# Two-stage kernel on one core (windowed attention, then a gated feed-forward): the loads of the first quad and of the first global rows

## The chip, the cores and the metric

The kernel runs on 1 core of one Trainium2 chip. The time is the device time of one execution in microseconds (us); the time before is the median of 3 runs. One further execution was profiled, and every view below is of that one.

A core has five engines that work side by side, each in its own program order: PE (TensorE, matmul; the loading of the stationary operand is shown apart, as PEld), DVE (VectorE), ACT (ScalarE), POOL (GpSimd) and SP (SyncE). They meet only at semaphores. Transfers between HBM and the on-chip memory are issued from SP, ACT or POOL and carried out by 16 DMA engines. The profile calls the queue of the transfers that POOL issues q0 ("software_dynamic"), that of SP q1 and that of ACT q10 (both "hardware_dynamic"). Only transfers issued from POOL change the type on the way here (f32 in HBM, bf16 on chip); those from SP and ACT bring f32 as it is.

## The reference, cut to what matters

```python
# q_l, k_l, v_l: (8, 8, 512, 64); q_g, k_g, v_g: (8, 8, 32, 64); all f32
def _attn_ref(q_l, k_l, v_l, q_g, k_g, v_g):
    k_all = np.concatenate([k_g, k_l], axis=2)
    v_all = np.concatenate([v_g, v_l], axis=2)
    out_g = np.matmul(sm(scale * q_g @ k_all.T), v_all)       # 32 global queries see every key
    mask = np.abs(pos[:, None] - pos[None, :]) <= 32          # local queries: a band of 65 keys
    s_ll = np.where(mask, scale * q_l @ k_l.T, -1e9)
    s_l = np.concatenate([scale * q_l @ k_g.T, s_ll], axis=-1)  # and the 32 global keys
    out_l = np.matmul(sm(s_l), v_all)
    return np.concatenate([out_g, out_l], axis=2)

def _moe_ref(x, w_in, w_out):                                 # x: (4352, 512)
    h = x @ w_in                                              # 512 -> 2048
    return (h / (1.0 + np.exp(-1.702 * h))) @ w_out           # 2048 -> 512
```

`sm` is a softmax over the last axis. The attention output, with the heads put side by side, is the input x of the feed-forward.

## The kernel before, in words

**Tiling.** The 8 batches are cut into 16 "quads" of four heads each: quad Q is batch Q // 2, heads 4(Q % 2) to 4(Q % 2) + 3. The first two quads (batch 0, called `a` and `c` in the code) are of class `Quad`, the other fourteen of class `Wide`. Per quad, k and q arrive as bf16 tiles `rk` and `rq` (128 x 1024), are turned on DVE by stream transposes into `kT` (`Tk`, L304 to L309) and a q tile `qt` (`Tq`, L311 to L313), and scores are made on PE (`S`). There are four such q tiles (`qtiles`, L181 to L186), each 128 x 24 x 32; the middle 16 of the 24 columns hold the local queries, and copies of the global queries are put into the outer columns by `ext` (L319 to L327). The class `Quad` has its own `ext`, with a switch that puts a copy on ACT instead of DVE; `Wide` has another one, which the change does not touch.

**The order of the work** is written out by hand: each engine does its instructions in the order in which the program makes them. For batch 0 that order is L653 to L737. In short, for quad a: scores of round 0 in two parts (`a.S(0, part=0)`, `part=1`), their exponential on ACT (`a.X(0)`, L387), round 1 (`a.S(1)`, `a.X(1)`, L382), then the transposes of quad c, its bias matmuls `c.B(0)` (L337), the products with global keys (`a.K`, `a.XK`, L373 and L418), `c.S(0)`, `c.X(0)`, the sums and products with v (`ekU`, `U`, L428 and L440), normalisation on DVE (`R`, `XL`, L464 to L473), and the same for c. Between them PE is given filler matmuls on a zeroed tile (`zero`, L648, and L179 at the start). When quad a's rows are normalised, the feed-forward of batch 0 begins (L713, `h_mm`, L588); it needs `w_in_sb`, which POOL loads in eight pieces (L256). From there the program alternates feed-forward (`h_step`, `o_mm`) with the attention of the next batch.

**The first loads.** Before the main order, each issuing engine gets its transfers, in this order:

- SP: global queries of batch 0 into `g32q` (L132, 64 KB, f32); the second half of quad 0's q into `early[:, 2]` (L146, 256 KB, f32); global keys into a buffer of their own, `g32k` (L132).
- ACT: quad 0's k in two halves into `early[:, 0:2]` (L144, 2 x 256 KB, f32).
- POOL: the first half of quad 0's q straight into `rq` (L145, 128 KB as bf16); the constant `step` by an `affine_select` (L153); then quad 1's k and q (`load(0, (1,), "kq")`, L81, 256 KB each as bf16), global values (L117, L118), the local values of batch 0 in four pieces (L243), some constants, and the weights (L256, L246).

The f32 pieces are turned into bf16 on chip: `cast_k` (L651) does the two halves of k on ACT, L658 the half of q on ACT, and `cast_g32` (L135) the global queries and keys on DVE. The casts and transposes in the hand-written order are L653 to L665: k on ACT; global queries on DVE (cast, then `transpose_g`, L237); the first two of quad a's four `ext` copies on ACT; q's half on ACT; `a.Tk` in two halves, `a.Tq` in two halves, the other two `ext` copies, and the cast and transpose of the global keys, all on DVE. Quad c's `Tk`, `Tq` and its four `ext` copies on DVE follow at L678 to L681.

The tile `early` is used once more, from L724 on, as the place of a tanh of the feed-forward.

Of the kernel before, what the change touches and what calls it, by code (L numbers as in the profile page):

```python
# [12 lines left out]
F32 = mybir.dt.float32  # L13
BF16 = mybir.dt.bfloat16
FP8 = mybir.dt.float8e4
AF = mybir.ActivationFunctionType
# [4 lines left out]
def kernel(  # L21
# [12 lines left out]
    nc = tc.nc  # L34

    B, H, Sl, D = q_l.shape
# [12 lines left out]
    TB = 512  # L49
# [7 lines left out]
    consts = ctx.enter_context(tc.tile_pool(name="consts", bufs=1))  # L57
    wts = ctx.enter_context(tc.tile_pool(name="wts", bufs=1))
    ld = ctx.enter_context(tc.tile_pool(name="ld", bufs=3))
# [6 lines left out]
    qf = q_l.rearrange("b (u j) (r t) d -> b (j r) u (t d)", j=4, t=16)  # L66
    kf = k_l.rearrange("b (u j) (r t) d -> b (j r) u (t d)", j=4, t=16)
    qgf = q_g.rearrange("b (u j) s d -> (j s) (b u) d", j=4)
    kgf = k_g.rearrange("b (u j) s d -> (j s) (b u) d", j=4)
# [4 lines left out]
    def load(b, us=(0, 1), names="qk"):  # L74
        if b not in loaded:
            loaded[b] = (ld.tile([128, 2, 16 * D], BF16, name="rk"),
                         ld.tile([128, 2, 16 * D], BF16, name="rq"))
        s = slice(us[0], us[-1] + 1)
        for name in names:
            dst, src = ((loaded[b][0], kf), (loaded[b][1], qf))[name == "q"]  # L80
            nc.gpsimd.dma_start(out=dst[:, s], in_=src[b][:, s])  # L81
# [34 lines left out]
    def load_turned(eng, out_, in_):  # L116
        eng.dma_start(out=out_[32:128], in_=in_[0:96])  # L117
        eng.dma_start(out=out_[0:32], in_=in_[96:128])  # L118
# [5 lines left out]

    g32 = {}

    def load_g32(name, src):
        t = g32[name] = consts.tile([128, 2, D], F32, name="g32%s" % name)
        if name == "v":
            load_turned(nc.sync, t, src[:, 0:2, :])  # L130
        else:
            nc.sync.dma_start(out=t, in_=src[:, 0:2, :])  # L132

    def cast_g32(name, t):
        nc.vector.tensor_copy(t[:, 0:2, :D], g32[name])  # L135

    load(0, names="")
    rk, rq = loaded[0]
    early = ld.tile([128, 4, TB], F32, name="early", bufs=1)
    k32 = early[:, 0:2].rearrange("p a b -> p (a b)")  # L140
    halves = (slice(0, 8 * D), slice(8 * D, 16 * D))
    load_g32("q", qgf)
    for f in halves:
        nc.scalar.dma_start(out=k32[:, f], in_=kf[0][:, 0, f])  # L144
    nc.gpsimd.dma_start(out=rq[:, 0, halves[0]], in_=qf[0][:, 0, halves[0]])  # L145
    nc.sync.dma_start(out=early[:, 2], in_=qf[0][:, 0, halves[1]])  # L146
    load_g32("k", kgf)

    warm = consts.tile([128, 512], BF16)
    nc.vector.memset(warm, 0.0)  # L150
# [3 lines left out]
        out=step, in_=step, pattern=[[1, 289]], compare_op=ALU.is_ge,  # L154
        fill=0.0, base=-97, channel_multiplier=-1,
    )
    ones32 = consts.tile([128, 32], BF16)
    bd = consts.tile([128, 4, 32], BF16)
    for i in range(2):
# [21 lines left out]
    qtiles = []  # L181
    for i in range(4):
        qt = consts.tile([128, 24, 32], F32, name="q%d" % i)
        nc.vector.memset(qt[:, 0:4, :], 0.0)
        nc.vector.memset(qt[:, 20:24, :], 0.0)
        qtiles.append(qt)  # L186

    qgT = consts.tile([128, NQ, 40], F32)
# [44 lines left out]
    def transpose_g(lo, hi, names="qk"):  # L233
        for name, dst, s in (("q", qgT, rqg), ("k", kgT, rkg)):
            if name not in names:
                continue
            nc.vector.transpose(dst[:, lo:hi, :32], s[:, lo:hi].bitcast(F32))  # L237
# [404 lines left out]
    pts, th4s = {}, {}  # L642

    a, c = Quad(0), Quad(1)
# [2 lines left out]
        for _ in range(n):  # L647
            nc.tensor.matmul(ps[:m, :w], lhsT=warm[:, :m], rhs=warm[:, :w], start=False, stop=False, skip_group_check=True)  # L648

    def cast_k(f):  # L650
        nc.scalar.activation(rk[:, 0, f], k32[:, f], AF.Copy)  # L651

    cast_k(halves[0])  # L653
    cast_k(halves[1])
    cast_g32("q", rqg)
    transpose_g(0, 2, "q")
    a.ext((0, 1), True)
    nc.scalar.activation(rq[:, 0, halves[1]], early[:, 2], AF.Copy)  # L658
    a.Tk(0, 8)
    a.Tk(8, 16)  # L660
    a.Tq(0, 8)
    a.Tq(8, 16)
    a.ext((2, 3))
    cast_g32("k", rkg)
    transpose_g(0, 2, "k")  # L665
    load_rest()
# [9 lines left out]
    zero(16, a.bk[1][3], 32, 32)  # L676
    a.X(1)
    c.Tk()  # L678
    c.ext((0, 1))
    c.Tq()  # L680
    c.ext((2, 3))  # L681
    c.B(0)
    a.K()
    a.XK()
# [36 lines left out]
            h_mm(0, fc, bank(pt, fc), (kc,))  # L721
    a.G()
    c.Gm()
    th4 = th4s[0] = early  # L724

    def tanh2(hf):
        f = slice(2 * hf, 2 * hf + 2)
# [16 lines left out]
    a, c = nq[1]  # L744
# [41 lines left out]
    a, c = nq[2]  # L786
# [122 lines left out]
```

## Time and profile before

| what | us |
|---|---|
| median of 3 runs | 299.23 (299.15 to 299.37) |
| the profiled execution, device time | 299.14 |
| its span, first to last instruction | 297.4 |
| PE busy in the span | 289.9 |
| DVE busy | 218.7 |
| ACT busy | 165.5 |
| POOL busy | 81.9 |

The granted TensorE clock is 1.0 over the whole span. Busy PE time includes the filler matmuls. In the timeline view a row is: start in us, length in us, engine, source line, operation, output <- inputs, shape, how many, and in brackets the idle time of the engine before it and what ended that. In the DMA view a queue's row is: packets, MB, and the time its packets took as a share of 16 engines in the stretch that was asked for; "to landing" is from the start of the issuing instruction to the moment the transfer is complete. Landings of the first transfers, as that view and the rows of single tiles give them (us after the issue, issue time in brackets):

| transfer | issued | to landing |
|---|---|---|
| k half 0, ACT, 256 KB f32 | 0.82 | 3.0 |
| global queries, SP, 64 KB f32 | 0.82 | 3.1 |
| q second half, SP, 256 KB f32 | 1.34 | 4.8 |
| global keys, SP, 64 KB f32 | 1.84 | 5.9 |
| q first half, POOL, 128 KB bf16 | 1.32 | 5.4 |
| quad 1's k, POOL, 256 KB bf16 | 2.48 | 5.7 |
| quad 1's q, POOL, 256 KB bf16 | 3.04 | 6.5 |

### The profile page before, as it was taken

The page shows a single profiled execution, that of the slowest core. Times are in us where ns is not written, and L with a number is a line of the kernel's source. Part 1 is how long each engine was busy: PE and PEld are TensorE (multiplying, and loading weights), DVE is VectorE, ACT ScalarE, POOL GpSimd, SP SyncE. Part 2 cuts the span into 40 slices and gives each one's busy share as a digit, 9 for nine tenths or more (in the row PEclk, how much of TensorE's full clock was granted, in tenths as well). Part 3 has the DMA queues.
Part 4 walks back from the last instruction along what each step waited for, and adds up shares of the span by engine and source line. Part 5 has one row for each costly group of instructions (what it writes and reads, how often), then busy time and mean ns, then how long its engine had stood idle before and what let it go on. Part 6 is the DMA issues. An engine that isn't in the chain of part 4 may idle for free.

```text
span 297.4 us, 8162 instructions
## 1 busy us (share of the span) xinstructions
PE 289.9 (97%) x3403; PEld 149.8 (50%) x3444; DVE 218.7 (74%) x440; ACT 165.5 (56%) x252; POOL 81.9 (28%) x133
## 2 busy tenths in 40 slices
PE   8999999999999999999999999999999999999995
PEld 4544446445454455445454455445544455445653
DVE  6679888979867887778877887788878866683320
ACT  4827465585556745576447654666546651663421
POOL 8884630589565002700072003500000000000000
PEclk9999999999999999999999999999999999999999
DMA  7999994596999613961299115901130022101122
GB/s 177 178 206 211 204 160 86 119 138 100 192 212 160 124 37 68 150 122 29 47 96 178 29 41 87 109 0 39 36 72 2 2 48 63 35 2 35 35 66 78
DMA packets 59316, 28.06 MB, mean 94 GB/s; under 512 B 47376, under 2 KB 49808, under 8 KB 59280
## 3 DMA queue, kind: packets, MB, share of 16 engines
q0 software_dynamic: 51728, 17.70, 53.1%
q1 hardware_dynamic: 7264, 9.31, 12.3%
q8 instruction: 27, 0.44, 0.6%
q10 hardware_dynamic: 288, 0.52, 0.5%
q14 instruction: 9, 0.07, 0.1%
HBM read 36.31 MB, written 8.91 MB: 152 GB/s over the span
## 4 chain that ended last, share of the span: by engine, by line
PE 92%; POOL 3%; DMA 3%; issue 1%; ACT 0%; POOLq 0%
PE op L613 39%; PE hp L588 38%; PE s L533 6%; PE ov L559 5%; DMA w_in_sb<-in_moe_w_in_dram 3%; PE s L588 1%; PE op L625 1%; POOL v L243 1%; PE og L570 1%; POOL w_in_sb L256 0%; PE s L559 0%; POOL rq L145 0%; POOL rvg L117 0%; PE og L458 0%; POOL rvg L118 0%
## 5 line engine op out<-in xcount | busy, mean ns | idle before, releaser
L613 PE MATMUL op<-w_out_sb,gT 128*128 128x512 bf16 x497 | 119.4, 379 | 1.8 <-issue 0.3
L596 DVE SCALAR_TENSOR_TENSOR gT<-th,hp 128x512 bf16<-128x512 f32 (+1 forms) x140 | 91.0, 656 | 39.7 <-ACT th L595 38.7
L588 PE MATMUL hp<-xL,w_in_sb 128*128 128x512 bf16 x488 | 108.4, 379 | 0.4
L595 ACT ACTIVATE th<-hp 128x512 f32<-128x512 f32 (+1 forms) x140 | 79.8, 573 | 43.0 <-PE hp L588 41.1
L588 PEld LDWEIGHTS <-w_in_sb 128*128 128x128 bf16 x576 | 56.1, 98 | 64.2 <-issue 0.5
L613 PEld LDWEIGHTS <-gT 128*128 128x128 bf16 x528 | 49.3, 98 | 54.9
L544 ACT ACTIVATE e<-s 128x1016 bf16<-128x1016 f32 (+1 forms) x56 | 53.3, 1005 | 7.4 <-PE s L533 7.1
L628 ACT ACTIVATE ob<-op 128x512 f32<-128x512 f32 x32 | 18.9, 599 | 62.3 <-PE op L613 62.3
L97 POOL DMA_DIRECT2D v<-in_v_l_dram x35 | 28.1, 806 | 82.1 <-PE og L570 74.0
L549 DVE TENSOR_TENSOR e<-e,mask 128x1712 bf16<-128x1712 bf16 (+1 forms) x27 | 28.4, 1051 | 3.4 <-ACT e L544 3.4
L464 DVE STREAM_TRANSPOSE sT<-ov 128x512 f32<-128x512 f32 x15 | 10.7, 716 | 14.4 <-PE ov L559 12.6
L473 DVE TENSOR_TENSOR xL<-ov,rs 128x512 bf16<-128x512 f32 x30 | 19.4, 686 | 1.9 <-PE ov L440 0.5
L533 PE MATMUL s<-q,kT 32*128 32x160 bf16 (+3 forms) x672 | 19.2, 243 | 0.0
L533 PEld LDWEIGHTS <-kT 32*128 32x128 bf16 x672 | 13.1, 94 | 12.0 <-issue 6.9
L507 DVE STREAM_TRANSPOSE kT<-rk 128x512 f32<-128x512 f32 x14 | 14.5, 1035 | 0.7 <-DMA rk<-in_k_l_dram 0.7
L99 POOL DMA_DIRECT2D v<-in_v_g_dram x24 | 14.1, 586 | 0.6 <-issue 0.5
L468 DVE STREAM_TRANSPOSE rs<-rT 128x512 f32<-128x512 f32 x16 | 11.4, 711 | 0.6
L559 PE MATMUL ov<-e,v 128*32 128x128 bf16 (+3 forms) x624 | 11.7, 223 | 0.0
L312 DVE STREAM_TRANSPOSE q<-rq 128x512 f32<-128x512 f32 (+1 forms) x17 | 11.4, 672 | 0.1
L559 PEld LDWEIGHTS <-v 128*32 128x32 bf16 x672 | 10.5, 97 | 0.0
L588 PE MATMUL hp<-xG,w_in_sb 128*128 128x256 bf16 x64 | 9.6, 273 | 0.1
L81 POOL DMA_DIRECT2D rk<-in_k_l_dram x10 | 6.4, 639 | 2.6 <-DMA w_out_sb<-in_moe_w_out_dram 2.0
(103 smaller groups left out, 158.8 us busy)
## 6 DMA issues: line engine op xcount, KB each, us to landing
out_dram<-ob SPq DMA_DIRECT2D x128, 64.0 KB, 1.8
v<-in_v_l_dram POOLq DMA_DIRECT2D x28, 96.0 KB, 4.8
rq<-in_q_l_dram POOLq DMA_DIRECT2D x5, 512.0 KB, 6.5
rk<-in_k_l_dram POOLq DMA_DIRECT2D x5, 512.0 KB, 8.5
w_in_sb<-in_moe_w_in_dram POOLq DMA_DIRECT2D x8, 256.0 KB, 8.6
w_out_sb<-in_moe_w_out_dram POOLq DMA_DIRECT2D x4, 512.0 KB, 11.1
v<-in_v_l_dram POOLq DMA_DIRECT2D x11, 128.0 KB, 6.4
rk<-in_k_l_dram POOLq DMA_DIRECT2D x5, 256.0 KB, 9.1
```

The source lines that it names most:

```text
L97: nc.gpsimd.dma_start(out=vt[0:n, :, c, :D], in_=vs[FIRST[c] : FIRST[c] + n])
L473: nc.vector.tensor_mul(self.x[:, 2 * self.u + h, :], self.st[1 + h], self.st["rs"])
L507: nc.vector.transpose(flat[:, 0:Sl].rearrange("p (r t) -> p t r", t=16), loaded[self.b][0][:, self.u].bitcast(F32))
L533: nc.tensor.matmul(bank(self.ps, j)[:, at : at + n], lhsT=self.k[p, KEYS[c] : KEYS[c] + 128, e], rhs=self.q[p, lo:hi, r0 : r0 + nr, e], st ...
L544: nc.scalar.activation(self.E[rnd][:, 2 * i : 2 * i + 2, :n], self.ps[i][:, :, :n], AF.Exp, scale=scale)
L549: eng.tensor_mul(e, e, mask[:, rnd : rnd + 1, :n].to_broadcast([128, 4, n]))
L559: nc.tensor.matmul(ov[32 * j : 32 * j + 32, :].rearrange("p (t r) -> p t r", t=16)[:, t0:t1, r0 : r0 + nr], lhsT=lv, rhs=self.E[rnd][:, j, ...
L588: nc.tensor.matmul(hp[:, : width(i)], lhsT=w_in_c[:, fc // 8, kc, fc % 8 // 2, :, fc % 2], rhs=(xL[i] if i < B else xG)[:, kc, :], start=( ...
L595: nc.scalar.activation(th[:, :n], hp[:, :n], AF.Tanh, scale=0.851)
L596: nc.vector.scalar_tensor_tensor(gTs[i][:, fc, :n], in0=th[:, :n], scalar=1.0, in1=hp[:, :n], op0=ALU.add, op1=ALU.mult)
L613: nc.tensor.matmul(op, lhsT=gTs[i][:, fc, tci * 128 : tci * 128 + 128], rhs=w_out_sb[:, fc, :], start=(first and fc == 4 * f4), stop=(fc = ...
L628: nc.scalar.activation(ob, op, AF.Copy, scale=0.5)
```

## The change

Quad 0's k is loaded by POOL in one transfer with the cast to bf16, ahead of everything else on POOL; its q by POOL in two halves, right behind the `affine_select`. The f32 detours in `early`, the transfers on ACT's queue and the three casts on ACT go. Global queries and keys share one f32 buffer, `stage`: the transfer of the keys is issued on SP only after the cast of the queries, since it overwrites what that reads. The eight `ext` copies of quads a and c are done on ACT, all of them ahead of quad a's transposes in program order; `a.Tk` is one transpose instead of two halves. The eight memsets of the q tiles' outer columns on DVE go. `early` is allocated later, for the tanh alone.

```diff
+    stage = consts.tile([128, 2, D], F32, name="stage")
+
     def load_g32(name, src):
-        t = g32[name] = consts.tile([128, 2, D], F32, name="g32%s" % name)
-        if name == "v":
-            load_turned(nc.sync, t, src[:, 0:2, :])
-        else:
-            nc.sync.dma_start(out=t, in_=src[:, 0:2, :])
+        g32[name] = stage
+        nc.sync.dma_start(out=stage, in_=src[:, 0:2, :])
...
-    early = ld.tile([128, 4, TB], F32, name="early", bufs=1)
-    k32 = early[:, 0:2].rearrange("p a b -> p (a b)")
     halves = (slice(0, 8 * D), slice(8 * D, 16 * D))
+    load(0, (0,), "k")
     load_g32("q", qgf)
-    for f in halves:
-        nc.scalar.dma_start(out=k32[:, f], in_=kf[0][:, 0, f])
-    nc.gpsimd.dma_start(out=rq[:, 0, halves[0]], in_=qf[0][:, 0, halves[0]])
-    nc.sync.dma_start(out=early[:, 2], in_=qf[0][:, 0, halves[1]])
-    load_g32("k", kgf)
...
         fill=0.0, base=-97, channel_multiplier=-1,
     )
+    for f in halves:
+        nc.gpsimd.dma_start(out=rq[:, 0, f], in_=qf[0][:, 0, f])
...
-        nc.vector.memset(qt[:, 0:4, :], 0.0)
-        nc.vector.memset(qt[:, 20:24, :], 0.0)
...
-    def cast_k(f):
-        nc.scalar.activation(rk[:, 0, f], k32[:, f], AF.Copy)
-
-    cast_k(halves[0])
-    cast_k(halves[1])
     cast_g32("q", rqg)
+    load_g32("k", kgf)
     transpose_g(0, 2, "q")
-    a.ext((0, 1), True)
-    nc.scalar.activation(rq[:, 0, halves[1]], early[:, 2], AF.Copy)
-    a.Tk(0, 8)
-    a.Tk(8, 16)
+    a.ext(act=True)
+    c.ext(act=True)
+    a.Tk()
     a.Tq(0, 8)
     a.Tq(8, 16)
-    a.ext((2, 3))
     cast_g32("k", rkg)
     transpose_g(0, 2, "k")
     load_rest()
...
     c.Tk()
-    c.ext((0, 1))
     c.Tq()
-    c.ext((2, 3))
...
-    th4 = th4s[0] = early
+    th4 = th4s[0] = ld.tile([128, 4, TB], F32, name="early", bufs=1)
```

## The prediction

> **What bounds the kernel now.** I read first the page's busy times, then the chain of waits of the first 24 us, then PE and PEld around the start of the feed-forward, then the timeline of the first 16 us, then the DMA view in narrow stretches.
>
> ```profile
> PE 289.9 (97%) x3403; PEld 149.8 (50%) x3444; DVE 218.7 (74%) x440; ACT 165.5 (56%) x252; POOL 81.9 (28%) x133
> ```
>
> PE is busy nearly throughout. In the order of the chain the feed-forward follows without a long hole from 18.44 us on; what comes before it is partly filler matmuls. So the time is: the moment at which the feed-forward of batch 0 starts, plus a fixed rest. All the edits lie ahead of that moment. The chain of waits says who sets it:
>
> ```profile
> 9.23 1.36 POOL w_in_sb L256 x2
> 10.59 7.73 DMA w_in_sb<-in_moe_w_in_dram
> 18.32 0.12 issue
> 18.44 1.67 PE s L588 x7
> ```
>
> By this, a weight transfer does. The timeline of PE and PEld says otherwise:
>
> ```profile
> 17.79 0.49 PE L440 MATMUL ov<-e,v 128*32 128x160 bf16 x16
> 18.21 1.41 PEld L588 LDWEIGHTS <-w_in_sb 128*128 128x128 bf16 x8
> 18.44 1.67 PE L588 MATMUL s<-xL,w_in_sb 128*128 128x512 bf16 x7 [0.16 <-DMA w_in_sb<-in_moe_w_in_dram]
> ```
>
> The weights are read by LDWEIGHTS, and the first of these starts at 18.21, before the landing at 18.32 that is said to release it. Eight are loaded and seven matmuls recorded: one record is missing, and the 0.16 us "wait" is its place. The attention matmuls end at 18.28 (17.79 + 0.49), and the feed-forward joins on. Of the eight weight pieces the third landed at 18.32; the first, which the first eight matmuls need, was issued at 9.18 and landed 6.6 us later, at 15.8. So the attention of quads a and c sets the start, with 2.4 us of cover over the weights. What paces that attention is seen here:
>
> ```profile
> 1.32 0.70 POOL L145 DMA_DIRECT2D rq<-in_q_l_dram  x1 [0.80 <-POOLq L893]
> ...
> 6.87 0.81 DVE L312 STREAM_TRANSPOSE q<-rq 128x256 f32<-128x256 f32 x2
> ...
> 8.03 0.92 PE L354 MATMUL s<-q,kT 32*128 32x80 bf16 x32
> ...
> 8.37 1.01 DVE L308 STREAM_TRANSPOSE kT<-rk 128x512 f32<-128x512 f32 x1
> 8.49 1.66 ACT L387 ACTIVATE e<-s 128x856 bf16<-128x856 f32 x2 [1.29 <-PE s L354]
> ...
> 10.04 1.82 ACT L382 ACTIVATE e<-s 128x428 bf16<-128x428 f32 x4
> ...
> 11.69 0.66 ACT L418 ACTIVATE ek<-kb 128x512 bf16<-128x512 f32 x1
> ...
> 12.25 1.66 ACT L387 ACTIVATE e<-s 128x856 bf16<-128x856 f32 x2
> ...
> 15.14 1.66 ACT L387 ACTIVATE e<-s 128x856 bf16<-128x856 f32 x2 [0.66 <-PE s L354]
> ```
>
> From a.X(0) at 8.49 ACT goes from exponential to exponential; its one wait (0.66 us) is for scores whose PSUM banks the previous exponential frees, so it shifts along. a.X(0) waits for quad a's scores, these for q's transposes (6.87 to 7.68), and these for q's first half, landed 1.32 + 5.4 = 6.7. **A shift of a.X(0) is a shift of the end, one for one.**
>
> **The change, part by part.**
>
> *POOL's first transfer.* It becomes k (256 KB as bf16) in place of half of q. When do its packets start? In the DMA view, for 1.3 to 4.75 us and then 4.75 to 4.8 us:
>
> ```profile
> q10 hardware_dynamic: 279, 0.52, 45.8%
> q1 hardware_dynamic: 357, 0.24, 29.5%
> ...
> q1 hardware_dynamic: 6, 0.01, 63.1%
> q0 software_dynamic: 2, 0.00, 24.0%
> ```
>
> No q0 packet until 4.75: 3.4 us after the issue at 1.32. Later issues into an empty queue are quicker: 55.96 to a first packet after 57.15 and before 57.25 (1.25 us), 68.66 to 70.1 or a little later (1.45), 116.94 to 118.4 (1.5). The early 2 us more are either a price of the first transfer of a run, which stays, or the work of the other queues, which goes. I take the first: at 118 to 118.5 the other queue's share was 58% and the delay was still 1.5 us, and up to 4.75 the two other queues together took 75%, so the engines had room. Ends for this unknown: first packet at 1.32 + 1.25 = 2.6 and at 4.75; chosen 4.75.
>
> The Trainium skill, "DMA: Bandwidth & Descriptors", section Specifications, gives about 1 us to the first byte on GpSimd's path, with no extra for the first transfer. The trace's first transfer disagrees (3.4 us) and its later ones nearly agree; by the rule k would start at some 2.3 us and the change would be a gain, rival 1 below.
>
> *Landing of quad 0's k and q.* The 256 KB issued at 55.96 landed 3.5 us later, 2.2 us after its first packet: k at 4.75 + 2.2 = 6.95. Behind it q0 works in order. Quad 1's k and q, 256 KB each, landed at 2.48 + 5.7 = 8.2 and 3.04 + 6.5 = 9.5, 1.3 us apart; so 0.65 us for each half of q: 7.6 and 8.25. Their issues cost POOL some 0.57 us each (0.59 and 0.56 at L81) and end near 3.7, before the queue moves.
>
> *DVE.* One Tk of 1.01 us (the row at 8.37): 7.0 to 8.05. Tq is 0.81 for two halves: the first to 8.45, the second, on land at 8.25, to 8.86. Before, Tq ended at 7.68 and a.X(0) began 0.81 later; now 8.86 + 0.81 = 9.67. **9.67 - 8.49 = +1.2 us.** Splitting k's arrival from its transpose no longer overlaps: before, half of Tk ran at 4.51 while the other half was on the way.
>
> *ACT's casts* (three of 0.61 to 0.63 us, ended 7.2) go; they stood ahead of Tk and Tq, and their gain is inside the times above. *ext*: eight copies on ACT at 0.2 us (0.41 for two at 6.27) are 1.6 us from about 4.6, over long before 9.67: nothing, as ACT is idle there; without that cover they would cost 1.6. DVE loses 0.50 + 0.21 + 0.41 = 1.1 us of copies behind Tq, of use only to quad c, whose scores wait for PSUM banks: nothing. *Memsets*: eight of 0.17 at 1.49 to 2.65; `ident` behind them waits for POOL's `step` anyway (2.56): nothing.
>
> *Global keys in the shared buffer.* SP issues them after the cast of the queries (3.99 + 0.32 = 4.3), not at 1.84. Ends for the landing: 3.1 us (the queries) and 5.9 (the keys before): 7.4 to 10.2. On DVE the cast stands behind Tq, at 8.86; behind it wait the transposes of quad c. At 10.2 kgT is ready at 10.2 + 0.39 + 0.24 = 10.8 and c.Tq at 10.8 + 1.01 + 0.71 = 12.55; c.S(0) is due at 11.55 + 1.2 = 12.75. Covered at both ends, by 0.2 us at the worse. I take 8.5, between the two rows, as the queue is less crowded than for 5.9.
>
> *POOL's queue behind.* Two more transfers stand ahead of quad 1's k and q, the values and the weights. By the steps above quad 1's q lands at 8.25 + 2 x 1.3 = 10.85, 1.35 later than before; c.Tq from 10.9 to 11.6, before 12.75. The q0 transfers from 5 to 24 us follow each other without a hole, so the first weight piece is 1.35 later too: 17.2, against a use at 18.2 + 1.2 = 19.4. The tightest user after that, c's keys of batch 1, was landed at 37.7 and waited for by DVE (0.7 us), but its scores run on PE at 42.5.
>
> **Sum.** Casts, copies, memsets, keys, weights 0; first quad's loads +1.2. Span 297.4 + 1.2 = 298.6; with the 1.74 us around the span (299.14 - 297.4) 300.3; that execution was 0.09 under the median: **300.4 us**. A price of the first transfer that is 0.3 smaller or a slower step of 0.1 us in each of four pieces moves it to 300.1 or 300.8.
>
> **Rivals.**
>
> 1. *The early start* (faster). The 2 us were the other queues' work. First packet at 2.6 to 2.8, k at 4.9, q at 5.55 and 6.2 (POOL's issues end at 3.7, so the queue is fed); Tk 5.0 to 6.0, Tq to 6.85, a.X(0) at 7.65: -0.8 us, 298.4. For it: the first q0 packets come just when ACT's queue runs dry (11% at 4.5 to 5). Against: q1 and q10 shared the engines from 3 us on, each with 30 to 70%, so one queue does not shut out another. The Trainium skill, same page, section "Queues, rings and completion order", says that an engine goes round the queues that have work; by that rule this rival falls, and the trace agrees for q1 and q10. It decides if the first packet is before 3.0.
> 2. *Half of it* (no change). The first packet at 3.0 to 4.1: every step above moves with it, and the shift is between -0.6 and +0.6; at 3.6, 299.3. For it: both causes may hold in part.
> 3. *The keys' buffer decides* (slower). An early start as in 1, but the keys land at 10.2 (with q0 at full load, as the 5.9 us row had it): quad c's Tq then ends at 12.55 and c.S(0) starts at about 12.85 instead of 11.55: +1.3, 300.5. It decides once the keys land later than 8.9. Against it: in that row they stood behind 256 KB of their own queue.
> 4. *The page's chain is right and the weights set the start.* With the forecast's queue they come 1.35 later: 300.6, in the forecast's own range.
>
> **Chances.** Forecast, with 4: 66%, own range 299.9 to 301.0. Rival 1: 12%, rival 2: 15%, rival 3: 7%. A measurement here can tell about 0.2%, 0.6 us. Slower 0.66 + 0.07 = 0.73 less 0.02 for a forecast that comes out under 0.6; same 0.17; faster 0.12. The range 298.9 to 301.1 leaves out rival 1 and a small upper tail.
>
> **What would show it.** After: no q0 packet before about 4.7; k's landing near 7, q's halves near 7.6 and 8.25; one Tk after it, a.X(0) near 9.7; the keys' cast without a long wait; first L588 LDWEIGHTS near 19.4, right after attention's last matmul. Wrong if q0 starts before 4.1, if a.X(0) moves without the feed-forward moving as much, or if DVE sits waiting for the keys.

## The result, and the profile after

The changed kernel takes 303.42 us (median of 4 runs, 302.74 to 304.59); the kernel before takes 299.19 (median of 4). The ratio is 1.0146, interval 1.0112 to 1.0180: slower by 1.5%, where 300.4 was forecast. The profiled execution took 303.72 with a span of 302.0 against 297.4.

The page's busy times and granted clock (one digit for each of 40 slices of 7.5 us):

```profile
PE 292.0 (97%) x3403; PEld 150.5 (50%) x3444; DVE 217.4 (72%) x425; ACT 165.1 (55%) x255; POOL 83.1 (28%) x135
...
PEclk9689999999999999999999999999999999999999
```

Nearly as much work as before in a longer span, and in the second and third slice PE did not have its full clock. It had it everywhere in the profile before. Rows from the timeline of the stretch up to the feed-forward, in order of time, those left out not marked one by one (start, length, engine, line; idle time before it and what ended that):

```profile
1.33 0.70 POOL L81 DMA_DIRECT2D rk<-in_k_l_dram  x1 [0.81 <-POOLq L878]
3.69 0.40 SPq L131 DMA_DIRECT2D stage<-in_k_g_dram  x1
5.38 1.04 DVE L301 STREAM_TRANSPOSE kT<-rk 128x512 f32<-128x512 f32 x1 [1.44 <-DMA rk<-in_k_l_dram]
7.06 0.45 DVE L305 STREAM_TRANSPOSE q<-rq 128x256 f32<-128x256 f32 x1 [0.63 <-DMA rq<-in_q_l_dram]
8.51 0.45 DVE L305 STREAM_TRANSPOSE q<-rq 128x256 f32<-128x256 f32 x1 [1.01 <-DMA rq<-in_q_l_dram]
9.46 1.66 ACT L380 ACTIVATE e<-s 128x856 bf16<-128x856 f32 x2 [4.13 <-PE s L347]
10.50 0.33 DVE L134 CAST rkg<-stage 128x128 bf16<-128x128 f32 x1 [1.54 <-DMA stage<-in_k_g_dram]
11.16 0.24 PE L366 MATMUL s<-qgT,kgT 32*32 32x32 bf16 x8 [1.22 <-DVE kgT L230]
11.73 1.60 PE L641 MATMUL s<-warm 128*128 128x512 bf16 x18 [0.33 <-issue]
13.27 1.35 PE L330 MATMUL s<-bias,ident 128*128 128x160 bf16 x8
14.55 1.04 PE L366 MATMUL kb<-q,kgT 32*32 32x512 bf16 x8
16.45 1.66 ACT L380 ACTIVATE e<-s 128x856 bf16<-128x856 f32 x2 [0.21 <-PE s L347]
...
22.58 1.41 PEld L581 LDWEIGHTS <-w_in_sb 128*128 128x128 bf16 x8
```

Before, the turned keys, their product and the bias matmuls stood here:

```profile
8.20 0.24 DVE L237 STREAM_TRANSPOSE kgT<-rkg 128x64 f32<-128x64 f32 x1
...
8.88 0.22 PE L373 MATMUL s<-qgT,kgT 32*32 32x32 bf16 x8
...
10.28 0.78 PE L337 MATMUL s<-bias,ident 128*128 128x160 bf16 x8
```

Four things are to be seen. Quad a's first exponential starts at 9.46 instead of 8.49: +0.97, about the forecast's 1.2 (in a second profile of the same kernel, e7 below, it starts at 8.76, so this shift is that of one execution). The cast of the global keys waits 1.54 us on DVE for its transfer, issued at 3.69 and landed at 10.47. PE stands before the product of global queries and keys (L366, 11.16; before: 8.88) until that cast and its transpose are done, with everything behind it. And from the product to quad c's first exponential (16.45; before: 12.25) it takes 5.29 us instead of 3.37, though the same instructions run: the eight bias matmuls take 1.35 us where they took 0.78. The windows view says why. Three stretches after, then the first of them before (us; busy time of PE, PEld, DVE, ACT and POOL, each with the number of instructions in brackets; granted clock, DMA share, GB/s):

```profile
6.80:10.20 3.40, 1.99 (x66) 1.46 (x66) 0.89 (x2) 0.73 (x1) 2.86 (x7) 1.00 1.22 181
10.20:13.60 3.40, 2.11 (x29) 1.25 (x31) 2.21 (x5) 2.44 (x6) 3.17 (x9) 0.50 2.35 159
13.60:17.10 3.50, 3.50 (x51) 1.39 (x49) 0.00 (x0) 1.54 (x3) 3.35 (x6) 0.51 1.40 199
```

```profile
6.80:10.20 3.40, 3.03 (x92) 2.08 (x93) 3.27 (x12) 2.10 (x4) 3.21 (x13) 1.00 1.64 179
```

PE was busy for 1.99 us of the first stretch, 3.03 before, and then worked at half clock for 6.8 us. The clock fell at 10.2, 0.3 us into PE's wait for the keys (9.94 to 11.16); the other holes ahead of the fall are the waits of 0.47 and 0.68 us for q's two halves. So the sum for the start of the feed-forward (18.21 before, 22.58 after, +4.37) is: first exponential +0.97; wait for the keys +1.31 (from that exponential to the product 1.70 us, 0.39 before); half clock +1.92 (5.29 less 3.37, an excess that e5 below shows to be the clock's); a remainder of 0.17. Everything after it is shifted by 4.4 us, up to PE's last group of matmuls (290.37 before, 294.76 after); the span grew by 4.6.

### The profile page after: what moved, and what is told of

It reads as the page before. It is cut to its first block, busy times and chain, and to the rows that moved or that the text cites. A ratio compares the mean times of both kernels' runs of the same rounds, so it can differ in the third digit from the quotient of the medians.

```text
span 302.0 us, 8146 instructions
## 1 busy us (share of the span) xinstructions
PE 292.0 (97%) x3403; PEld 150.5 (50%) x3444; DVE 217.4 (72%) x425; ACT 165.1 (55%) x255; POOL 83.1 (28%) x135
## 3 DMA queue, kind: packets, MB, share of 16 engines
HBM read 36.31 MB, written 8.91 MB: 150 GB/s over the span
## 4 chain that ended last, share of the span: by engine, by line
PE 85%; DMA 10%; issue 1%; POOL 1%; ACT 0%; POOLq 0%
PE op L606 38%; PE hp L581 34%; PE s L526 6%; PE ov L552 5%; DMA w_out_sb<-in_moe_w_out_dram 5%; DMA w_in_sb<-in_moe_w_in_dram 2%; DMA v<-in_v_g_dram 2%; DMA rq<-in_q_l_dram 2%; PE op L618 1%; PE og L563 1%; PE s L552 0%; POOL v L236 0%; POOL rk L81 0%; POOL w_in_sb L249 0%; POOL rq L151 0%
## 5 line engine op out<-in xcount | busy, mean ns | idle before, releaser
L81 POOL DMA_DIRECT2D rk<-in_k_l_dram x11 | 7.2, 651 | 3.3 <-DMA w_out_sb<-in_moe_w_out_dram 1.9
```

## Experiments

Two theories were set against each other: K, the late keys starve PE and its clock halves; L, the late halves of q do that, and the keys add little. All times are medians in us; "before" is the kernel before on the same chip in the same session. The ratio with its interval is the one on record, not the quotient of the two medians. Then, from the one profiled execution of each kernel: start of a.X(0); start of the product of global queries and keys; start of c.X(0); whether the clock fell. The last column counts the timed executions with half clock in them: each lists its mean granted clock, and that is either 0.998 and more or 0.994 and less. (A piece of 3.4 us at half clock, as the profiles show them, takes 0.006 off the mean over some 300 us.)

| kernel | time | before | ratio (interval) | a.X(0) | product | c.X(0) | clock fell | executions with half clock |
|---|---|---|---|---|---|---|---|---|
| before | | | | 8.49 | 8.88 | 12.25 | no | 22 of 75 |
| changed | 303.42 | 299.19 | 1.0146 (1.0112 to 1.0180) | 9.46 | 11.16 | 16.45 | yes | 4 of 4 |
| e1: keys' own buffer | 300.40 | 299.56 | 1.0015 (0.9988 to 1.0042) | 9.46 | 9.86 | 13.22 | no | 3 of 10 |
| e2: before, shared buffer | 303.60 | 299.56 | 1.0124 (1.0074 to 1.0173) | 9.28 | 11.11 | 15.99 | yes | 4 of 4 |
| e3: filler at the keys | 303.41 | 299.56 | 1.0102 (1.0068 to 1.0136) | 10.29 | 12.51 | 15.88 | no | 3 of 8 |
| e4: before, copies and memsets | 299.25 | 299.56 | 0.9981 (0.9955 to 1.0006) | 8.91 | 9.31 | 12.68 | no | 1 of 10 |
| e5: filler in all waits | 301.63 | 299.38 | 1.0078 (1.0043 to 1.0114) | 9.29 | 10.98 | 14.35 | no | 1 of 10 |
| e6: e2 with that filler | 301.22 | 299.38 | 1.0044 (1.0020 to 1.0069) | 9.13 | 10.71 | 14.07 | no | 0 of 10 |
| e7: changed, again | 303.37 | 299.38 | 1.0102 (1.0074 to 1.0129) | 8.76 | 10.95 | 15.59 | yes | 10 of 10 |
| e8: product after bias | 300.21 | 299.38 | 1.0018 (0.9991 to 1.0044) | 8.40 | 10.75 | 12.49 | no | 3 of 10 |

The kernel before, then, has half clock in some executions too, 22 of the 75 of these sessions (on the chip of e5 to e8 those took 300.55 to 301.66 us, the others 299.08 to 299.81); the changed kernel had it in all 14.

**e1, the keys in a buffer of their own**, in the changed kernel:

```diff
+    stage_k = consts.tile([128, 2, D], F32, name="stagek")
     def load_g32(name, src):
-        g32[name] = stage
-        nc.sync.dma_start(out=stage, in_=src[:, 0:2, :])
+        t = g32[name] = stage_k if name == "k" else stage
+        nc.sync.dma_start(out=t, in_=src[:, 0:2, :])
...
     load_g32("q", qgf)
+    load_g32("k", kgf)
...
     cast_g32("q", rqg)
-    load_g32("k", kgf)
```

> The changed kernel, but the global keys keep a buffer of their own and are issued on SP at the start, right behind the queries. Theory K (the keys, issued at 3.69 and landed at 10.47, leave PE without work, and PE's clock then halves): the keys land before 7, no wait for them on DVE, no half clock, and what is left is the late first quad, +1.0: 300.2 us. Theory L (the halves of q, landed at 7.03 and 8.49, are late, and PE's waits for them are what halves the clock; the keys add little): the clock still halves near 10.2, 302 to 303 us.

Measured 300.40. Rows of its timeline, at the same places:

```profile
8.66 0.31 DVE L136 CAST rkg<-stagek 128x128 bf16<-128x128 f32 x1
...
9.46 1.66 ACT L383 ACTIVATE e<-s 128x856 bf16<-128x856 f32 x2 [4.28 <-PE s L350]
9.86 0.22 PE L369 MATMUL s<-qgT,kgT 32*32 32x32 bf16 x8
```

The keys, issued at 1.34, landed at 5.72; no wait for them; from product to c.X(0) 3.36 us (9.86 to 13.22), as before the change. The whole of this execution is shifted by +0.97, the shift of its first exponential. It is the same shift as in the changed kernel by another way: here quad a's k was the late piece (landed at 6.93 instead of 5.36), and q's halves had no wait of their own. On the time K holds: without the shared buffer the medians differ by 0.8 us (by the interval, -0.4 to +1.3). On the clock this one profile does not test L, since q's halves left no holes apart in it; the ten executions do, with half clock in 3, about as often as before the change.

**e2, the shared buffer alone**, in the kernel before: `load_g32("k", kgf)` moved behind `cast_g32("q", rqg)`, both into one tile.

> The kernel before, with one edit alone: global keys and queries share one buffer, so the keys are issued after the cast of the queries. Theory K: the keys land at 9 to 10.5, PE waits about 1 us or more for them, the clock halves for some us, 301 to 302.5 us. Theory L: the wait costs 0 to 0.8 us, the clock stays at 1.0, 299.2 to 300.0 us.

Measured 303.60: this one edit makes the whole loss. The keys were issued at 4.34 and landed at 10.39, and PE stands before their product:

```profile
11.11 0.24 PE L374 MATMUL s<-qgT,kgT 32*32 32x32 bf16 x8 [1.15 <-DVE kgT L238]
```

The time is above K's 301 to 302.5; and in this profile the clock fell at 8.2, ahead of the wait for the keys, in a stretch in which quad a's k came late. So holes that quad a's pieces leave have a part in when the clock falls, and what of the half clock the keys alone bring is not separated.

**e3, filler at the wait for the keys:**

```diff
             if split:
+                zero(8, ps[3])
                 self.gk(ps[2][:, RW : RW + 32], self.qg)
```

> The changed kernel with eight more filler matmuls (128x512, of zeros) on PE ahead of the product of global queries and keys, where PE waits from 9.94 to 11.16. It takes no wait away, it only gives PE work in it. Theory K: PE is busy through that wait, the clock stays at 1.0 and the time falls to 300.5 to 301.5 us (the waits themselves stay). Theory L: the stretch that is judged lies before 10.2 and has the waits for q in it; the clock halves all the same, 303 us or more.

The profile has the full clock, and again 3.37 us from product to c.X(0) (12.51 to 15.88). But the time is 303.41, as L expected: in this execution q's second half landed at 9.30, 0.8 us later than in the changed kernel's profile, the eight fillers outlasted the wait for the keys (kgT was ready at 12.10), and POOL's later transfers, held up too, brought some weights late (the last shift is +4.2, that of c.X(0) +3.6). Of the eight timed executions five have no half clock (301.17 to 303.75 us) and three have it (303.36 to 304.48): the filler takes it away in part, as K expected, but the time does not show what that is worth.

**e4, the edits beside the loads:** copies on ACT and no memsets, in the kernel before.

> The kernel before, with the edits that leave the loads alone: the eight copies of global queries on ACT and no memsets of the q tiles. Both theories: they stand beside other work, 299.0 to 299.4 us, and the clock stays at 1.0. If either edit has a share in the loss: above 299.8 us.

299.25, ratio 0.9981 with 1 in the interval: no share in the loss, as forecast.

**e5 and e6, filler in all three waits**, of the changed kernel and of e2, sized to the waits (the changed kernel was run again beside them, as e7):

```diff
     zero(8, a.bk[1][3], 32, 32)
+    zero(2, a.bk[1][3])
...
     zero(10, a.bk[1][3], 32, 32)
+    zero(3, a.bk[1][3])
...
             if split:
+                zero(5, ps[3])
                 self.gk(ps[2][:, RW : RW + 32], self.qg)
```

> The changed kernel with full-size filler matmuls (128x512, of zeros) in all three places where PE waits in its profile: 2 ahead of the first part of quad a's scores, 3 ahead of the second, 5 ahead of the product of global queries and keys (0.4, 0.6 and 1.1 us at full clock, about the waits' length). If the half clock is a cost of its own (1.9 us, from the stretch between that product and quad c's first exponential, 5.29 us with the half clock and 3.37 without): clock 1.0, 301 to 302 us. If the half clock only fills waiting time: 303 us or more.

> The kernel before with the shared buffer alone, and the same fillers. If the half clock is a cost of its own: clock 1.0, 301 to 302 us instead of 303.6. If not: 303 us or more.

> The changed kernel again, for comparison on the same chip: 302.5 to 304.5 us.

301.63 and 301.22, against 303.37 for the changed kernel on the same chip; all three are inside what was expected. (e2, which e6 fills, took 303.60 on another chip.) Useless work in the waits makes the kernel 1.7 us faster. In e5's profile the clock is whole and the matmuls short again:

```profile
10.98 0.22 PE L367 MATMUL s<-qgT,kgT 32*32 32x32 bf16 x8
...
13.10 0.63 PE L367 MATMUL kb<-q,kgT 32*32 32x512 bf16 x8
...
14.35 1.66 ACT L381 ACTIVATE e<-s 128x856 bf16<-128x856 f32 x2
```

From product to c.X(0) it takes 3.37 us again. So the half clock is a cost of its own, and the waits remain.

**e8, another order on PE.** The keys are issued as late as in the changed kernel. On PE only the product moves; the call of a.X(1), which reads it, moves along, but ACT's order stays:

```diff
-            if split:
-                self.gk(ps[2][:, RW : RW + 32], self.qg)
...
     zero(3, a.bk[1][3])
     zero(16, a.bk[1][3], 32, 32)
-    a.X(1)
     c.Tk()
     c.Tq()
     c.B(0)
+    a.gk(a.bk[1][2][:, RW : RW + 32], a.qg)
+    a.X(1)
```

> The changed kernel with the late keys as they are, but the product of global queries and keys stands in PE's order behind the fillers and quad c's bias matmuls, instead of ahead of them (the exponentials of quad a's second round move with it). If the keys cost by what is queued behind that product on PE: PE has no wait from 9.9 to 11.2, the wait's 1.3 us and most of the half clock come back, 300.3 to 301.5 us. If the keys cost by what is queued behind their cast on DVE (quad c's transposes): 302.5 us or more.

Measured 300.21, at the lower edge of the first expectation. The timeline of the profiled execution, which with 299.61 was the fastest of the ten:

```profile
9.78 0.23 DVE L134 CAST rkg<-stage 128x128 bf16<-128x128 f32 x1 [1.89 <-DMA stage<-in_k_g_dram]
...
10.04 0.78 PE L330 MATMUL s<-bias,ident 128*128 128x160 bf16 x8
10.75 0.22 PE L364 MATMUL s<-qgT,kgT 32*32 32x32 bf16 x8
...
12.49 1.66 ACT L378 ACTIVATE e<-s 128x856 bf16<-128x856 f32 x2
```

DVE waits for the keys as before the move (1.89 us; 1.54 and 2.13 in the two profiles of the changed kernel), and quad c's transposes behind that cast are late too; it costs next to nothing here (c.X(0) at 12.49, 0.24 us later than before). It was PE's order that turned the late keys into lost time. From the medians of one chip: changed 303.37, filled 301.63, reordered 300.21, before 299.38. That is 1.7 us for the clock, 1.4 for PE's wait, 0.8 for the rest, in which the loads of quad a stand; the profile's sum had 1.92, 1.31 and 0.97 + 0.17. The medians of e5, e8 and before have some executions with half clock in them; of the others alone they are 301.50, 300.07 and 299.24, and the three parts 1.9, 1.4 and 0.8.

**e9 and e10, in search of a kernel that beats both.** e9 is the kernel before with e4's edits and e8's order; e10 is e9 with all of quad a's k and q by the queues of SP and ACT (and two of the copies back on DVE).

> The kernel before with its own loads and its own keys' buffer; copies on ACT, no memsets, and the product of global queries and keys behind quad c's bias matmuls. In the kernel before the keys were ready (8.44) before PE came to that product (8.88), so nothing should be won in an undisturbed run: 299.0 to 299.4 us. Theory K's reading of PE's order would allow a gain only in runs in which the keys land late.

> The kernel of e9, but all of quad 0's k and q by the queues of SP and ACT as f32 (k's first half and q's first half on ACT, the second halves on SP), cast on ACT; nothing of quad 0 on POOL. If the start of a loaded engine's second queue (2 us late in the kernel before) is what holds q's first half, this gets q 0.3 to 0.5 us earlier and the time to 298.7 to 299.0 us. If the casts on ACT (four of 0.62 us in a row) take the place of it: 299.2 to 299.8 us.

e9: 299.51 against 299.59, ratio 0.9996 (0.9968 to 1.0024): no gain, as expected, though 0.1 above the stated range. Its profiled execution (301.99) is one of 3 in 12 with half clock, and it shows that this needs no late keys: the second half of quad a's k, on ACT's queue, was waited for until 7.40, PE waited 2.54 us for q, and the clock fell at 8.76. e10: 302.31, ratio 1.0073 (1.0044 to 1.0102), above both figures, with half clock in 9 of 10 executions. Neither reason of the expectation was the one: in its profile ACT's cast of q's second half waited 1.29 us for a transfer issued at 1.83 and landed at 8.14, and the clock halved for 3.4 us after it. Why the fourth piece on these queues took 6.3 us was not tried. No version that beats the kernel before was found.

## Why the prediction was wrong

**The step that failed** is *Global keys in the shared buffer*, with its "covered at both ends, by 0.2 us at the worse" and its price of nothing. Three parts of it fell:

- Its upper end. The landing was bounded by 5.9 us; it took 6.8 (3.69 to 10.47). The choice of 8.5, "as the queue is less crowded than for 5.9", had the queue of SP in mind, and it was the engines that were crowded: in the DMA view, queues from 3.7 to 6 us and from 6 to 6.5 us,

```profile
q0 software_dynamic: 247, 0.31, 94.6%
...
q0 software_dynamic: 73, 0.07, 98.9%
q1 hardware_dynamic: 32, 0.01, 11.8%
```

  SP's queue has not one packet until 6, 1.9 us after its issuing instruction ended (4.09), and then crawls beside q0.
- What is queued behind the wait. The forecast followed the cast on DVE to quad c's transposes, which do have slack (e8). It did not follow kgT to PE, where the product stands ahead of 19 fillers, quad c's bias matmuls and `a.K`. The slack there is small: in the kernel before PE came to the product at 8.88, with kgT ready at 8.44 (8.20 + 0.24). So kgT could be later by 0.44 us and the shift of a.X(0), 1.4 us in all, before PE waits; it was later by 2.67 (8.44 to 11.11). The due time of c.S(0) has no part in that.
- The clock. The forecast took PE's waits at their length. With q's two halves apart (PE waits 0.47 and 0.68 us for them) and 1.22 us for the keys, PE had half its clock for 6.8 us, and that cost 1.9 us. No step priced that.

**What bounds the kernel: right.** The feed-forward's first LDWEIGHTS follows attention's end (22.16 + 0.49 against 22.58), and the first weight piece landed at 16.22; its start and PE's last group of matmuls moved by the same 4.4 us. So rival 4, the weights, falls too. **"A shift of a.X(0) is a shift of the end": wrong as the only path.** It holds where the keys are early (e1: +0.97 and +0.97), but a second path to c.X(0) leads through kgT and PE.

**The first transfer on POOL: the shift near by luck, the reason wrong.** The forecast took the 3.4 us to the first q0 packet for a price of the run's first transfer. In the changed kernel the queue's rows for 1.3 to 2.5 us and 2.5 to 3 us are

```profile
q1 hardware_dynamic: 268, 0.06, 23.8%
...
q0 software_dynamic: 6, 0.01, 43.8%
q1 hardware_dynamic: 4, 0.00, 0.8%
```

so q0 starts at 2.85, 1.5 us after its issue: rival 1's condition. It is so in all six profiles without quad a's loads on SP and ACT (2.83 to 2.87); in the six with them it is 4.71 to 4.90. So the delay goes with the other queues' work and not with being the first; whether q0 had packets to offer while it stood still no view shows. The Trainium skill, "DMA: Bandwidth & Descriptors", section "Queues, rings and completion order", has an engine go round its queues packet by packet; these starts disagree with it as it was read in rival 1, since a queue that joined loaded engines had no packet for about 2 us. Yet the gain of rival 1 did not come: k landed at 5.36, but q's halves at 7.03 and 8.49, 1.7 and 1.5 us after the piece ahead of them where 0.65 was forecast for each. In the executions profiled the second half landed anywhere from 7.4 (e8) to 9.3 us (e3). So +0.97 came out near the forecast's +1.2 by two errors against each other, an earlier start and slower steps; that is luck, and in e7, the same kernel, the shift was +0.27.

**Copies, memsets, weights: right** (e4; first weight piece 6.4 us ahead of its use).

**The rivals.** Rival 3, with 7%, had the mechanism: early start, keys landing above 10.2, the shared buffer decides. It put the price in the wrong queue (DVE) and without the clock: +1.3 where the keys and the clock cost 3.2. All three signs of being wrong that the forecast named came: q0 before 4.1 (2.85), a.X(0) moving without the feed-forward moving as much (0.97 against 4.37), and DVE waiting for the keys (1.54).

## What to carry to other kernels

When an edit puts a wait ahead of a transfer, follow the data to every engine that uses it, and on each look at what stands behind the first user in that engine's order; here DVE, the first reader, could wait almost for nothing, and PE, one step further, could not. A shared buffer turns a load at the start into one that joins DMA engines already full: it was issued 1.9 us later than before and landed 2.7 us later. And price a wait of PE near a thin stretch with the clock it may cost, which here was more than the wait (1.9 us against 1.3); reordering one product behind work that was ready won back most of the loss.

## What the runs showed of the hardware that had not been expected

PE's clock fell to half not after an idle stretch but in a busy one with holes: PE was busy 1.99 of 3.40 us in the stretch before it fell (the changed kernel), 1.65 of 3.41 (e2), 1.88 of 3.41 (e10). The least busy of these stretches, with 1.01 and 1.10 us, are those of e7 and e9. How little is too little the runs do not settle: in e3 the clock stayed whole, although wherever one lays stretches of 3.41 us end to end over its profile, one of them has about 2.0 us or less. The half clock came in pieces of 3.41 us (one in e7, e9 and e10, two in the changed kernel and e2). The Trainium skill, "TensorE: Matmul & The Clock Gate", section "Part 1: The HAM clock gate", gives a window of 3413 ns, which the pieces agree with, and an idle window as the condition, which they do not.

In these first microseconds a transfer that joined loaded engines started late, on either kind of queue: q0 by 3.4 us instead of 1.5 behind the loads of SP and ACT, and SP's keys 1.3 to about 2 us after their issue ended behind q0 in the changed kernel, e3, e5, e7 and e8 (3.1 to 3.2 us in e2 and e6), where the first transfers of the run on ACT began 0.6 us after theirs. It is no rule for every load: in the kernel before, a transfer issued from POOL at 116.9 us began after 1.5 us beside a queue that took 38% of the engines meanwhile.
